# Attention and MLP steps of a chained kernel in a 3 to 2 pattern across block seams, with z of the next batch split two blocks ahead

## The chip, the cores and the metric

One core of one Trainium2 chip runs the whole program. The metric is the device time of one execution in microseconds (us). The engines are PE (TensorE matmuls; PEld is its weight load), DVE (VectorE), ACT (ScalarE), POOL (GpSimd) and SP (SyncE, which issues most DMAs here).

## The reference

Three layers are chained. Everything is float32.

```python
# attention: u, v (8, 3072, 256), z (8, 3072, 64)
attn = np.maximum(z @ z.T / S, 0.0) ** 2
x = u * (attn @ v)                       # then flattened to (24576, 256)
# MLP: w_in (256, 2048), w_out (2048, 256)
h = x @ w_in
x = (h * sigmoid(h)) @ w_out
# routed MLP: 8 experts, w1 (256, 1024), w2 (1024, 256); each row goes to the expert with the largest logit
e = argmax(x @ w_gate); p = softmax(x @ w_gate)[e]
out = p * sigmoid(x @ w_output_gate)[e] * (relu(x @ w1[e]) @ w2[e])
```

## The kernel before

Float32 products are made of three matmuls on split operands: hi is a rounded copy of a tile, lo is what is left, and hi x hi, hi x lo and lo x hi are added up in PSUM. So nearly every tile costs a copy (hi, on ACT mostly) and a subtraction (lo, on DVE).

The 24576 rows are 48 blocks of 512 (TQ). Block n is block q = n % 6 of batch b = n // 6. An **attention block** has 24 steps, one per 128 keys (KT = 24); an **MLP block** has 16 steps, one per 128 hidden columns (NF1 = 16). Step i is an `Item` with a front, which makes hi and lo of its tile, and a back, which multiplies them into an accumulator. The loop at the end of `moe_chain` emits front(i), the lo of step i - 1, and back(i - 3) (LOOK = 3), so PE's order in the program is: front of a step, back of the step three earlier.

A **direct** attention step has two front matmuls (L264, L265), relu (L267), square (L269) and a copy to hi (L271 on ACT or L273 on DVE), lo (L242), and six back matmuls (L289 to L291). The scores are symmetric, so from block 3 on a block q with q > 0 need not compute the tiles against earlier blocks of its batch: such a **mirrored** step loads the stored tile `sym` with four DMAs (L216), transposes it in 32 x 32 blocks on DVE (L223), copies hi (L259) and subtracts lo (L242); it has no front matmul. A direct step whose tile will be needed later stores it to `sym` (L230). An MLP step has six front matmuls (L323), sigmoid (L325, ACT), product (L327, DVE), hi (L330), lo (L332) and twelve back matmuls of 256 columns (L357 to L359).

After the last back of an attention block, `finish` (L302, two instructions) multiplies the accumulator by u into x, and `split_x` makes xh and xl of it (L195, L197). The MLP block n needs both, and the attention block n + 1 needs nothing of them.

The order of steps is written out by hand in the list `order`. From block 3 on it is: seven attention steps of block n (PRE), then sixteen times one MLP step of block n - 1 and one attention step of block n, then the last attention step. So at each seam of two blocks eight attention steps follow each other.

Beside the steps there are tasks: each has a step by which it is due, a step from which it may run, and a cost; `run_tasks` emits a task when it is due, or earlier when the steps' budgets leave credit. Tasks split z and v of a batch (`prep`: hl, hh and ll, vh and vl), transpose mirrored tiles, decode the MLP weights during blocks 0 to 2, and route the rows of a finished MLP block: 32 dot products of 256 columns (L367, each with a read of the accumulator), a selection (L399 to L414), a rank (L425 to L430) and four scatters. Loads for `prep` and for mirrored tiles go through four buffers `raw`, in the order in which the tasks are due, and SP issues all of them.

```python
prep(max(att_step(n, j * NS) - (0 if n else 2), rel), rel, load_zz(b, j), f_hl(j))
prep(att_step(n, 0), att_step(n - 1, KT // 2) if n else 0, load_zz(b, q), f_hh((b, q)))
```

After block 47 come 61 tiles of the routed MLP (L637, L656 and the back matmuls again), which the change leaves as they are but for buffers.

Of the kernel before, what the change touches and what calls it, by code (L numbers as in the profile page):

```python
# [29 lines left out]
PRE = 7  # L30

# [10 lines left out]
def moe_chain(tc, zT, uT, vp, win, wout, w12, wgT, wogT, out):  # L42
# [20 lines left out]
    assert NBLK > 3 and KT >= PRE + NF1 and KT > 2 * PRE and NF1 >= 16 and NA <= P and NB <= P and N // P <= 256  # L63
# [3 lines left out]
    with ExitStack() as ctx:  # L67
# [37 lines left out]
        ident = cp.tile([P, P], F32, name="ident")  # L105
        make_identity(nc, ident)
# [77 lines left out]

        def split_x(b, q, last=False):
            x = xs[(b, q)]
            if last:
                r = mk(cp, [P, NS, RW], F32, "rec", 2).rearrange("p s c -> p (s c)").bitcast(F32R)
                h = [r[:, c * TQ:(c + 1) * TQ] for c in range(ND)]
                l = [mk(cp, [P, TQ], F32R, "x", 2) for c in range(ND)]  # L190
            else:
                h, l = ([t[:, c, :] for c in range(ND)] for t in [mk(cp, [P, ND, TQ], F32R, g, 1) for g in ("xh", "xl")])
# [27 lines left out]
        def flip(b, q, k):  # L220
            def f(t):
                a = flipped[b, q, k] = mk(cp, [P, TQ], F32, "t1", 3)
                nc.vector.transpose(a, t)  # L223
            return f
# [7 lines left out]
        def att_items(b, q, hold):  # L232
# [4 lines left out]
            def front(i):  # L237
# [39 lines left out]
            def back(i):  # L277
                k = ks[i]

                def f():  # L280
# [708 lines left out]
```

## Time and profile before

| what | us |
|---|---|
| median of 3 runs | 5383.55 (5381.29 to 5387.24) |
| the profiled execution's own time | 5386.84 |
| its span, first to last instruction | 5385.1 |
| busy: PE, PEld | 5237.8 (97%), 4536.8 (84%) |
| busy: DVE, ACT, POOL | 3830.7 (71%), 3233.8 (60%), 483.3 (9%) |
| granted TensorE clock, mean | 0.995 |

The span is the time from the first to the last instruction of the profiled execution. A busy time is the sum of the stretches in which at least one instruction of that engine ran. Matmuls overlap, so that PE's busy time is no measure of how densely they stand; the start times in the timeline are. "L290 [1.22 <-DVE lo L242]" behind a row means that the engine was idle for 1.22 us before that instruction, and that the last thing that it waited for was DVE's instruction of line 242.

### The profile page before, as it was taken

What the parts mean: (1) busy time and instruction counts of PE and PEld (TensorE: products, weight loads), DVE (VectorE), ACT (ScalarE), POOL (GpSimd) and SP (SyncE); (2) the same over time, 40 slices, a digit from 0 to 9 for tenths busy, and PEclk for the clock granted to TensorE, in tenths of its full rate; (3) what the DMA queues carried; (4) which work ended last, traced back from release to release, by engine and by line L of the source; (5) the groups of instructions that cost most, each with busy time, mean ns of one, the idle gap of its engine ahead of it and who ended that gap; (6) DMA issues with size and microseconds to landing.
All of it is one profiled execution on the core that took longest, in us unless ns stands there. A gap on an engine that the chain in (4) does not pass through costs nothing.

```text
span 5385.1 us, 88728 instructions
## 1 busy us (share of the span) xinstructions
PE 5237.8 (97%) x30026; PEld 4536.8 (84%) x30026; DVE 3830.7 (71%) x9655; ACT 3233.8 (60%) x5776; POOL 483.3 (9%) x503
## 2 busy tenths in 40 slices
PE   7999999999999999999999999999999999999999
PEld 5888888888878887888888888888888899999998
DVE  8777757776776667676767676677667886666687
ACT  6655665566556655656565556556665555555576
POOL 3100000000000000000000000000000022111111
PEclk9999999999999999999999999999999999999999
DMA  4143323433342334233423342334324456565564
GB/s 149 56 88 77 102 79 81 89 94 83 78 96 82 83 72 106 77 82 71 105 82 77 77 106 85 69 78 109 83 71 76 136 175 202 176 181 176 168 228 160
DMA packets 1335279, 574.38 MB, mean 107 GB/s; under 512 B 1173405, under 2 KB 1206814, under 8 KB 1319072
## 3 DMA queue, kind: packets, MB, share of 16 engines
q1 hardware_dynamic: 1316000, 516.72, 37.7%
q0 software_dynamic: 18816, 51.93, 2.6%
q8 instruction: 237, 3.88, 0.3%
q14 instruction: 226, 1.85, 0.1%
HBM read 391.32 MB, written 178.14 MB: 106 GB/s over the span
## 4 chain that ended last, share of the span: by engine, by line
PE 80%; DVE 9%; ACT 5%; DMA 3%; issue 2%; SPq 0%; DVEq 0%; ACTq 0%; POOL 0%; POOLq 0%
PE ps L323 17%; PE ps L656 10%; PE acc L357 10%; PE acc L359 10%; PE acc L358 10%; PE acc L290 7%; PE acc L291 6%; PE acc L289 6%; DVE lo L242 2%; PE ps L265 2%; PE ps L264 2%; ACT t L269 2%; DVE junk L367 1%; DVE t L223 1%; ACT t L267 1%
## 5 line engine op out<-in xcount | busy, mean ns | idle before, releaser
L327 DVE TENSOR_TENSOR t<-ps,t 128x512 f32<-128x512 f32 x768 | 531.0, 691 | 791.3 <-ACT t L325 756.3
L358 PE MATMUL acc<-woutl,hi 128*128 128x256 f32 x3600 | 1004.8, 279 | 0.0
L290 PE MATMUL acc<-lo,vh 128*128 128x512 f32 x2304 | 922.5, 400 | 82.8 <-DVE lo L242 82.6
L242 DVE TENSOR_TENSOR lo<-t,hi 128x512 fp32r<-128x512 f32 x1152 | 796.8, 693 | 249.9 <-ACT hi L271 249.9
L291 PE MATMUL acc<-hi,vl 128*128 128x512 f32 x2304 | 909.9, 395 | 0.0
L289 PE MATMUL acc<-hi,vh 128*128 128x512 f32 x2304 | 906.4, 393 | 0.0
L330 ACT ACTIVATE hi<-t 128x512 fp32r<-128x512 f32 x768 | 486.0, 633 | 661.8 <-DVE t L327 647.4
L359 PE MATMUL acc<-wouth,lo 128*128 128x256 f32 x3072 | 860.3, 280 | 12.2 <-DVE lo L332 12.1
L357 PE MATMUL acc<-wouth,hi 128*128 128x256 f32 x3072 | 860.1, 280 | 0.0
L325 ACT ACTIVATE t<-ps 128x512 f32<-128x512 f32 x768 | 456.7, 595 | 452.3 <-PE ps L323 450.1
L358 PEld LDWEIGHTS acc<-woutl,hi 128*128 128x128 f32 x3600 | 681.1, 189 | 38.2
L290 PEld LDWEIGHTS acc<-lo,vh 128*128 128x128 f32 x2304 | 435.6, 189 | 234.3 <-DVE lo L242 140.2
L357 PEld LDWEIGHTS acc<-wouth,hi 128*128 128x128 f32 x3072 | 579.6, 189 | 32.6
L359 PEld LDWEIGHTS acc<-wouth,lo 128*128 128x128 f32 x3072 | 583.1, 190 | 16.7 <-DVE lo L332 16.7
L323 PE MATMUL ps<-xl,winh 128*128 128x512 f32 x1504 | 596.3, 396 | 0.2
L323 PE MATMUL ps<-xh,winh 128*128 128x512 f32 x1504 | 592.0, 394 | 0.0
L323 PE MATMUL ps<-xh,winl 128*128 128x512 f32 x1504 | 590.7, 393 | 0.0
L367 DVE CUSTOM_DVE_ANT_0 junk<-rec,wg 128x256 f32<-128x256 f32 x1536 | 570.3, 419 | 0.0
L259 ACT ACTIVATE hi<-t 128x512 fp32r<-128x512 f32 x468 | 296.1, 633 | 427.0 <-DVE t L223 333.3
L433 POOL DMA_INDIRECT scr<-rec,si x192 | 200.8, 1046 | 3850.3 <-DVE si L430 1167.1
L332 DVE TENSOR_TENSOR lo<-t,hi 128x512 fp32r<-128x512 f32 x768 | 518.9, 676 | 24.5
L289 PEld LDWEIGHTS acc<-hi,vh 128*128 128x128 f32 x2304 | 435.8, 189 | 98.0
(444 smaller groups left out, 9770.5 us busy)
## 6 DMA issues: line engine op xcount, KB each, us to landing
raw<-in_w_dram SPq DMA_DIRECT2D x122, 1024.0 KB
sym<-t SPq DMA_DIRECT2D x468, 256.0 KB
raw<-sym SPq DMA_DIRECT2D x1872, 64.0 KB
raw<-in_zT_dram SPq DMA_DIRECT2D x192, 128.0 KB
raw<-in_vp_dram SPq DMA_DIRECT2D x96, 256.0 KB
u<-in_uT_dram SPq DMA_DIRECT2D x96, 256.0 KB
xg<-scr SPq DMA_DIRECT2D x39, 544.0 KB
x<-scr SPq DMA_DIRECT2D x304, 64.0 KB
```

Source lines behind the costliest of these rows:

```text
L242: nc.vector.tensor_tensor(out=lo, in0=a, in1=r32(hi), op=ALU.subtract)
L289: nc.tensor.matmul(acc[:, c, :], h, hi, start=i == 0, stop=False)
L290: nc.tensor.matmul(acc[:, c, :], h, lo, start=False, stop=False)
L291: nc.tensor.matmul(acc[:, c, :], l, hi, start=False, stop=i == KT - 1)
L323: nc.tensor.matmul(ps, win_at(w, c, f_), x[c], start=c == 0 and i == 0, stop=c == ND - 1 and i == 2)
L327: nc.vector.tensor_tensor(out=g, in0=ps, in1=sg, op=ALU.mult)
L332: return lambda: nc.vector.tensor_tensor(out=lo, in0=g, in1=r32(hi), op=ALU.subtract)
L357: nc.tensor.matmul(y[:, s, :], a, wh, start=first and s % per_bank == 0, stop=False, skip_group_check=True)
L358: nc.tensor.matmul(y[:, s, :], a, wl, start=False, stop=False, skip_group_check=True)
L359: nc.tensor.matmul(y[:, s, :], l, wh, start=False, stop=last, skip_group_check=True)
L367: nc.vector.tensor_tensor_reduce(out=j, in0=a, in1=w, scale=1.0, scalar=0.0, op0=ALU.mult, op1=ALU.add, accum_out=res)
L656: nc.tensor.matmul(ps[:, 0:T], w[:, o:o + P], y[c][:, 0:T], start=c == 0 and j == 0, stop=c == ND - 1 and j == 2)
```

## The change

The order from block 3 on is cut into eighths: three attention steps of block n, then two MLP steps, all through, also across the seams. The MLP of block n - 1 starts with the third eighth of block n and ends in the second eighth of block n + 1. So two x are held: even blocks split into xh and xl, odd ones into xo and x. In block 2 the MLP steps of block 1 are mixed 1 to 1. The last two eighths of block 47 have no MLP steps among them.

u is loaded into the tile xf ten steps before the block's end, and finish works in place. relu and square work in place in t1 (four buffers instead of three), t0 is left to sigmoid with one buffer. Of q = 0, a third of the copies to hi is made on DVE instead of half. hl of the next batch is due in blocks n - 2 (four of six), n - 1 and n; hh five steps before the block's first step; v one step earlier than before. The fill for padding is made in xl during block 0 and kept in DRAM (blank), and the identity for the routed MLP's transposes is made when its pool opens.

```diff
-                        later(2, 1.2, finish, 0)
-                        if hold != "held":
-                            later(3, 1.2, lambda: split_x(b, q, hold == "last"), 0)
+                        later(1, 1.2, finish, 0)
+                        later(3, 1.2, lambda: split_x(b, q, hold == "last"), 0)
...
-                h, l = ([t[:, c, :] for c in range(ND)] for t in [mk(cp, [P, ND, TQ], F32R, g, 1) for g in ("xh", "xl")])
+                odd = (b * NQ + q) % 2
+                h, l = ([t[:, c, :] for c in range(ND)] for t in
+                        [mk(ap_ if g == "xo" else cp, [P, ND, TQ], F32R, g, 1) for g in (("xo", "x") if odd else ("xh", "xl"))])
...
-                    r = mk(cp, [P, TQ], F32, "t0", 2)
-                    nc.scalar.activation(r, ps, AF.Relu)
-                    a = mk(cp, [P, TQ], F32, "t1", 3)
-                    nc.scalar.activation(a, r, AF.Square)
-                    if (early and q and k % 2) or (not early and (q or k % 2)):
+                    a = mk(cp, [P, TQ], F32, "t1", 4)
+                    nc.scalar.activation(a, ps, AF.Relu)
+                    nc.scalar.activation(a, a, AF.Square)
+                    if (early and q and k % 2) or (not early and (q or k % 3)):
...
-                    if i == LOOK + 1:
-                        st["u"] = []
-                        for c in range(ND):
-                            ut = mk(ap_, [P, TQ], F32, "u", 2)
-                            nc.sync.dma_start(out=ut, in_=uT[b, q, :, c, :])
-                            st["u"].append(ut)
+                    if i == KT - UAT:
+                        load_u(b, q)
...
             def finish():
-                x = xs[(b, q)] = []
-                for c in range(ND):
-                    x.append(mk(ap_, [P, TQ], F32, "raw", DEPTH) if hold == "last" else mk(cp, [P, TQ], F32, "x", 2))
-                    nc.vector.scalar_tensor_tensor(out=x[c], in0=st["acc"][:, c, :], scalar=AS, in1=st["u"][c], op0=ALU.mult, op1=ALU.mult)
+                for c, x in enumerate(xs[(b, q)]):
+                    nc.vector.scalar_tensor_tensor(out=x, in0=st["acc"][:, c, :], scalar=AS, in1=x, op0=ALU.mult, op1=ALU.mult)
...
-                    sg = mk(cp, [P, TQ], F32, "t0", 2)
+                    sg = mk(cp, [P, TQ], F32, "t0", 1)
...
+        def make_blank():
+            w = TB // P
+            t = r32(mk(cp, [P, ND, TQ], F32R, "xl", 1)).rearrange("p c t -> p (c t)")[:, 0:w * RW].rearrange("p (s c) -> p s c", c=RW)
+            nc.gpsimd.memset(t, 0.0)
+            nc.gpsimd.memset(t[:, :, D + E:D + E + 1], 1.0e6)
+            for dst in (blank, scr[E * CAP:E * CAP + TB, :]):
+                nc.sync.dma_start(out=dst.rearrange("(p s) c -> p s c", p=P), in_=t)
...
+        GA, GM = KT // 8, NF1 // 8
+        owed = []
         for n in range(3, NBLK):
-            order += [("a", n, 0, PRE)]
-            end = NF1 - (PRE if n == NBLK - 1 else 0)
-            for k in range(end):
-                order += [("m", n - 1, k, k + 1), ("a", n, PRE + k, PRE + k + 1)]
-            order += [("a", n, PRE + end, KT), ("m", n - 1, end, NF1)]
-        order += [("m", NBLK - 1, 0, NF1)]
+            for g in range(8):
+                if n > 3 or g >= 2:
+                    j = (g - 2) % 8 * GM
+                    owed.append(("m", n - 1 if g >= 2 else n - 2, j, j + GM))
+                if n < NBLK - 1 or g < 6:
+                    order += owed
+                    owed = []
+                order += [("a", n, g * GA, (g + 1) * GA)]
+        order += owed + [("m", NBLK - 2, 6 * GM, NF1), ("m", NBLK - 1, 0, NF1)]
...
-                    rel = last_use(n - 1, range(j * NS, (j + 1) * NS)) + 1 if n else 0
-                    prep(max(att_step(n, j * NS) - (0 if n else 2), rel), rel, load_zz(b, j), f_hl(j))
-            prep(att_step(n, 0), att_step(n - 1, KT // 2) if n else 0, load_zz(b, q), f_hh((b, q)))
+                    if n:
+                        due = att_step(n - 2, KT // 2 + 2 * j) if j < NQ - 2 else att_step(n - 1, KT // 2) if j < NQ - 1 else att_step(n, KT // 2)
+                        rel = max(last_use(n - t, range(j * NS, (j + 1) * NS)) for t in range(1, NQ + 1)) + 1
+                    else:
+                        due, rel = max(att_step(n, j * NS) - 2, 0), 0
+                    prep(due, rel, load_zz(b, j), f_hl(j))
+            prep(att_step(n, 0) - (5 if n else 0), att_step(n - 1, KT // 2) if n else 0, load_zz(b, q), f_hh((b, q)))
```

How the instructions move shows at three places.

**DVE at the seam of blocks 16 and 17**, before. L223 transposes a mirrored tile, L242 makes lo of an attention step, L302 is finish, L367 a dot product with its read, L197 makes xl:

```order
L223 STREAM_TRANSPOSE t_3866_15760<-raw_15169 128x512
L302 SCALAR_TENSOR_TENSOR x_15767<-acc_14763,u_14790 128x512
L302 SCALAR_TENSOR_TENSOR x_15769<-acc_14763,u_14792 128x512
L242 TENSOR_TENSOR lo_15733<-t_3859_15739,hi_15732 128x512
L367 ISA junk_15786,L_15751<-rec_15691,wg 128x256
L367 ISA L_15751 128x1
L367 ISA junk_15788,L_15751<-rec_15691,wg 128x256
L367 ISA L_15751 128x1
L223 STREAM_TRANSPOSE t_3876_15790<-raw_15217 128x512
L197 TENSOR_TENSOR xl_15798<-x_15767,xh_15797 128x512
L197 TENSOR_TENSOR xl_15798<-x_15769,xh_15797 128x512
L242 TENSOR_TENSOR lo_15776<-t_3866_15760,hi_15775 128x512
```

and in the changed kernel, where the lines are L303 (finish), L251 and L333 (lo of an attention and of an MLP step), L206 (xl), L328 (the MLP's product), and L426 to L431 are the rank of the rows of an earlier block:

```order
L333 TENSOR_TENSOR lo_16262<-t_3757_16259,hi_16261 128x512
L303 SCALAR_TENSOR_TENSOR xf_15823<-acc_15395,xf_15823 128x512 x2
L251 TENSOR_TENSOR lo_16272<-t_3763_16276,hi_16271 128x512
L426 TENSOR_TENSOR t_16314<-ps_16311,ecap 128x32
L427 TENSOR_TENSOR t_16314<-t_16314,oh_16220 128x32
L429 TENSOR_REDUCE sf_16317<-t_16314 128x4
L431 CAST si_16319<-sf_16317 128x4
L251 TENSOR_TENSOR lo_16290<-t_3767_16294,hi_16289 128x512
L206 TENSOR_TENSOR xl_16356<-xf_15823,xh_16355 128x512 x2
L328 TENSOR_TENSOR t_3780_16370<-ps_16361,t_3779_16368 128x512
L251 TENSOR_TENSOR lo_16334<-t_3775_16338,hi_16333 128x512
L328 TENSOR_TENSOR t_3786_16392<-ps_16383,t_3785_16390 128x512
```

Finish and xl stood among mirrored steps, two of their transposes and dot products; now they stand among direct steps and MLP products.

**DVE in a mirrored group of the changed kernel**, further on in block 17 (names as above, L232 is the transpose):

```order
L328 TENSOR_TENSOR t_3804_16479<-ps_16470,t_3803_16477 128x512
L251 TENSOR_TENSOR lo_16451<-t_3797_16443,hi_16450 128x512
L328 TENSOR_TENSOR t_3809_16500<-ps_16491,t_3808_16498 128x512
L333 TENSOR_TENSOR lo_16482<-t_3804_16479,hi_16481 128x512
L232 STREAM_TRANSPOSE t_3812_16512<-raw_16034 128x512
L333 TENSOR_TENSOR lo_16503<-t_3809_16500,hi_16502 128x512
L232 STREAM_TRANSPOSE t_3816_16529<-raw_16059 128x512
L251 TENSOR_TENSOR lo_16520<-t_3812_16512,hi_16519 128x512
```

Before, one product, one lo, one transpose and one lo followed each other in turn; now the second product stands ahead of the first MLP lo (L333).

**ACT at the seam of batches 2 and 3**, before. L168 and L174 make hl and hh of z, L95 vh of v, L259 hi of a mirrored step, L267 and L269 are relu and square of the new batch's first step:

```order
L330 ACTIVATE hi_17553<-t_4297_17551 128x512
L259 ACTIVATE hi_17568<-t_4300_17563 128x512
L259 ACTIVATE hi_17588<-t_4304_17584 128x512
L168 ACTIVATE hl_107<-raw_17482 128x512
L95 ACTIVATE vh_113<-raw_17524 128x512
L174 ACTIVATE hh_17607<-raw_17565 128x512
L267 ACTIVATE t_4316_17618<-ps_17615 128x512
L269 ACTIVATE t_4317_17620<-t_4316_17618 128x512
L95 ACTIVATE vh_114<-raw_17586 128x512
```

and in the changed kernel, with L173 (hh), L264 (hi, mirrored), L326 and L331 (sigmoid and hi of the MLP), L96 (vh), L272 and L273 (relu and square):

```order
L264 ACTIVATE hi_17039<-t_3938_17032 128x512
L173 ACTIVATE hh_17055<-raw_16919 128x512
L326 ACTIVATE t_3948_17072<-ps_17065 128x512
L331 ACTIVATE hi_17076<-t_3949_17074 128x512
L326 ACTIVATE t_3953_17093<-ps_17086 128x512
L331 ACTIVATE hi_17097<-t_3954_17095 128x512
L264 ACTIVATE hi_17111<-t_3957_17107 128x512
L264 ACTIVATE hi_17125<-t_3961_17121 128x512
L264 ACTIVATE hi_17153<-t_3969_17149 128x512
L96 ACTIVATE vh_108<-raw_17059 128x512
L326 ACTIVATE t_3975_17179<-ps_17172 128x512
L331 ACTIVATE hi_17183<-t_3976_17181 128x512
```

hl is gone from the seam. hh was the instruction just ahead of the first relu (L267); now twelve others stand between it and the first relu (L272), which follows the last row shown by two.

## Rows read from the trace of the kernel before

**Rows 1.** The page, part 1: busy time, share, instructions.

```profile
PE 5237.8 (97%) x30026; PEld 4536.8 (84%) x30026; DVE 3830.7 (71%) x9655; ACT 3233.8 (60%) x5776; POOL 483.3 (9%) x503
```

**Rows 2.** Windows, blocks 3 to 47: stretch, length, busy by engine, clock, DMA share, GB/s.

```profile
275.50:4200.00 3924.50, 3825.26 (x20679) 3251.33 (x20678) 2746.24 (x7000) 2368.74 (x3996) 193.71 (x225) 1.00 0.36 85
```

**Rows 3.** Chain of waits (start, length, what), then PE's timeline, in undisturbed stretches.

```profile
1342.65 1.39 PE ps L323 x6
1344.04 0.23 PE acc L289
...
1345.42 0.12 PE acc L357
...
1346.83 1.39 PE ps L323 x6
...
1697.99 1.37 PE ps L323 x6
...
1702.57 1.37 PE ps L323 x6
...
1588.29 0.39 PE L264 MATMUL ps<-hh,hl 128*128 128x512 f32 x1
...
1590.14 0.39 PE L264 MATMUL ps<-hh,hl 128*128 128x512 f32 x1
```

**Rows 4.** PE's timeline at the seam of blocks 14 and 15.

```profile
1330.48 0.39 PE L289 MATMUL acc<-hi,vh 128*128 128x512 f32 x1
1332.09 0.50 PE L290 MATMUL acc<-lo,vh 128*128 128x512 f32 x1 [1.22 <-DVE lo L242]
...
1336.45 0.40 PE L289 MATMUL acc<-hi,vh 128*128 128x512 f32 x1
1337.07 0.50 PE L290 MATMUL acc<-lo,vh 128*128 128x512 f32 x1 [0.22 <-DVE lo L242]
```

**Rows 5.** PE's timeline at the starts of batches 2 and 3.

```profile
1048.52 0.49 PE L264 MATMUL ps<-hh,hl 128*128 128x512 f32 x1 [2.41 <-DVE vl L93]
...
1571.69 0.39 PE L291 MATMUL acc<-hi,vl 128*128 128x512 f32 x1
1575.05 0.80 PE L264 MATMUL ps<-hh,hl 128*128 128x512 f32 x1 [2.98 <-ACT hh L174]
...
1576.37 0.41 PE L357 MATMUL acc<-wouth,hi 128*128 128x256 f32 x1
```

**Rows 6.** Chain of waits at the seam of blocks 14 and 15.

```profile
1330.27 1.17 DVE x L302 x2
...
1332.38 0.34 DVE junk L367
...
1333.35 1.18 DVE xl L197 x2
```

**Rows 7.** Timelines of PE and DVE behind the front of an MLP step.

```profile
1563.56 0.39 PE L289 MATMUL acc<-hi,vh 128*128 128x512 f32 x1
...
1564.44 0.69 DVE L327 TENSOR_TENSOR t<-ps,t 128x512 f32<-128x512 f32 x1 [1.70 <-ACT t L325]
1565.05 0.68 DVE L242 TENSOR_TENSOR lo<-t,hi 128x512 fp32r<-128x512 f32 x1
1565.65 0.70 DVE L223 STREAM_TRANSPOSE t<-raw 128x512 f32<-128x512 f32 x1
1566.28 0.65 DVE L332 TENSOR_TENSOR lo<-t,hi 128x512 fp32r<-128x512 f32 x1
```

**Rows 8.** Groups of ACT: line, count, busy us, mean ns, idle before and its end.

```profile
L269 ACT ACTIVATE t<-t 128x512 f32<-128x512 f32 x684 | 432.7, 633 | 44.8 <-DMA sym<-t 13.9 <-DVE lo L332 5.8 <-ACT t L267 2.3
L267 ACT ACTIVATE t<-ps 128x512 f32<-128x512 f32 x684 | 400.4, 585 | 38.1 <-PE ps L265 37.3
L271 ACT ACTIVATE hi<-t 128x512 fp32r<-128x512 f32 x564 | 356.9, 633 | 18.0
```

**Rows 9.** SP's timeline with a backlog of loads.

```profile
1333.78 11.04 SPq L216 DMA_DIRECT2D raw<-sym  x16
```

More of the change, by code (lines that the diff above doesn't have):

```diff
@@ L183, in moe_chain, with load_u @@
         xs = {}
+        def load_u(b, q):
+            t = mk(cp, [P, ND, TQ], F32, "xf", 1)
+            x = xs[(b, q)] = [t[:, c, :] for c in range(ND)]
+            for c in range(ND):
+                nc.sync.dma_start(out=x[c], in_=uT[b, q, :, c, :])
         def split_x(b, q, last=False):
@@ L344, in f @@
                         later(1, 0, copy(rec, 0), 0)
-                        later(2, 0, copy(rec, 2), 0)
+                        later(1, 0, copy(rec, 2), 0)
                 return f
@@ L498, in f @@
                 r = nc.sync.value_load(fr[0:1, e:e + 1], min_val=0, max_val=E * CAP - TB)
-                nc.sync.dma_start(out=scr[ds(r, TB), :].rearrange("(p s) c -> p s c", p=P), in_=fill)
+                nc.sync.dma_start(out=scr[ds(r, TB), :].rearrange("(p s) c -> p s c", p=P), in_=blank.rearrange("(p s) c -> p s c", p=P))
                 padded.append(e)
@@ L524, in final_tables @@
                 later(4 + NF2 * e, 0.0, pad(fr, e))
-        fill = cp.tile([P, TB // P, RW], F32, name="fill")
-        def make_fill():
-            nc.gpsimd.memset(fill, 0.0)
-            nc.gpsimd.memset(fill[:, :, D + E:D + E + 1], 1.0e6)
-            nc.sync.dma_start(out=scr[E * CAP:E * CAP + TB, :].rearrange("(p s) c -> p s c", p=P), in_=fill)
+        blank = dram.tile([TB, RW], F32, name="blank")
+        def make_blank():
[5 more added lines that the diff above has]
+                nc.sync.dma_start(out=dst.rearrange("(p s) c -> p s c", p=P), in_=t)
         bstack = ExitStack()
@@ L574, in f @@
                 r = nc.sync.value_load(tabs[kind][t:t + 1, 0:1], min_val=0, max_val=E * CAP + TB - T)
-                st["xb"] = [mk(cp, [P, TQ], F32, "x", 2) for _ in range(ND)]
+                t_ = r32(mk(cp, [P, ND, TQ], F32R, "x", 1))
+                st["xb"] = [t_[:, c, :] for c in range(ND)]
                 for c in range(ND):
@@ L636, in f @@
                     for s in range(T // P):
-                        nc.tensor.transpose(ps[:, s * P:(s + 1) * P], st["xg"][:, s, c * P:(c + 1) * P], ident)
+                        nc.tensor.transpose(ps[:, s * P:(s + 1) * P], st["xg"][:, s, c * P:(c + 1) * P], bp["i"])
                 split(ps[:, 0:T], st["yh"][c][:, 0:T], st["yl"][c][:, 0:T], m2_at[i])
@@ L694, in moe_chain @@
         blocks = [(b, q) for b in range(B) for q in range(NQ)]
-        order = [("a", 0, 0, KT), ("a", 1, 0, KT), ("a", 2, 0, PRE), ("m", 0, 0, NF1), ("a", 2, PRE, 2 * PRE), ("m", 1, 0, NF1), ("a", 2, 2 * PRE, KT)]
-        for n in range(3, NBLK):
-            order += [("a", n, 0, PRE)]
-            end = NF1 - (PRE if n == NBLK - 1 else 0)
-            for k in range(end):
-                order += [("m", n - 1, k, k + 1), ("a", n, PRE + k, PRE + k + 1)]
-            order += [("a", n, PRE + end, KT), ("m", n - 1, end, NF1)]
-        order += [("m", NBLK - 1, 0, NF1)]
+        order = [("a", 0, 0, KT), ("a", 1, 0, KT), ("a", 2, 0, PRE), ("m", 0, 0, NF1)]
+        for k in range(NF1):
+            order += [("a", 2, PRE + k, PRE + k + 1), ("m", 1, k, k + 1)]
+        order += [("a", 2, PRE + NF1, KT)]
+        GA, GM = KT // 8, NF1 // 8
+        owed = []
+        for n in range(3, NBLK):
+            for g in range(8):
[7 more added lines that the diff above has]
+        order += owed + [("m", NBLK - 2, 6 * GM, NF1), ("m", NBLK - 1, 0, NF1)]
         steps = {}
         for n, bq in enumerate(blocks):
-            steps["a", n] = att_items(*bq, {1: "held", NBLK - 1: "last"}.get(n))
+            steps["a", n] = att_items(*bq, "last" if n == NBLK - 1 else None)
             steps["m", n] = moe_items(*bq)
@@ L728, in prep, with used, last_use @@
             stream.append((due, rel, len(stream), load, use, since))
-        def last_use(n, keys):
+        def used(n, keys):
             o = key_order(*blocks[n])
             return max(att_step(n, o.index(k)) for k in keys)
+        def last_use(n, keys):
+            direct = [k for k in keys if not mirrored(*blocks[n], k)]
+            return used(n, direct) if direct else 0
         def f_hl(j):
@@ L795, in moe_chain @@
         tmp = wgt
-        t_val = tmp[:, 2 * TQ:3 * TQ], fill.rearrange("p s c -> p (s c)")[:, 0:TQ]
+        t_val = tmp[:, 2 * TQ:3 * TQ], mk(cp, [P, TQ], F32, "junk", 1)
         t_rem = tmp[:, 3 * TQ:4 * TQ]
```

27 lines of the change are left out of this document (14 added, 13 removed).

## The prediction

> **What bounds the kernel now.** I read the engines' busy times first, then the windows, then the timeline of PE and, where PE paused, that of DVE. PE is busy 97% of the span [rows 1]; the blocks in which attention and MLP steps run together take 3924.5 us of it and keep PE busy 3825.3 us at a granted clock of 1.00 [rows 2]. So PE is the bound, and what can be won is its pauses. A busy share hides part of them, because matmuls overlap (0.39 us long, 0.23 us apart); I count from start to start.
>
> The undisturbed pace: six MLP front matmuls, one mirrored attention step and the twelve MLP back matmuls repeat every 4.18 us (1342.65 to 1346.83), the mirrored step being 1.38 us of it (1344.04 to 1345.42) [rows 3]. With a direct step instead, the pair takes 4.58 us, and a direct step alone 1.85 us (1588.29 to 1590.14) [rows 3]. So an MLP step is 2.80 or 2.73 us of PE.
>
> The pauses stand in one place, the seam of two blocks, where eight attention steps follow each other without an MLP step. In the rows of one seam PE starts a matmul of L290 1.61 us after the one before it, and later another 0.62 us after, where 0.23 us is due; both wait for DVE's lo of L242 [rows 4]. That is 1.8 us, and about 2 with the slower matmuls behind each pause. At the seam of two batches it is worse: PE waits 3.36 us for hh, whose z was loaded too late, and the next two matmuls take 1.32 us instead of 0.46 [rows 5]: 4.0 us for that alone.
>
> One batch, from its first L264 to that of the next, is 1048.52 to 1575.05, 526.5 us [rows 5]. Its work is 96 MLP steps, 60 mirrored and 84 direct ones: 60 x 1.38 + 84 x 1.85 = 238.2, and 96 x 2.73 to 2.80 = 262.1 to 268.8 us. So PE loses 19.5 to 26.2 us per batch; weighted by partners it would be 23, and I take 22, as the pauses that I can point at are five of 2 and one of 4 or more. Seven whole batches (blocks 6 to 47) and the three seams of blocks 3 to 5 make 7 x 22 + 7 = **161 us**, in the range 143 to 190. The other pauses lie in blocks 0 and 1 and at the ends, where the order stays.
>
> **The change, part by part.**
>
> *Even mixing.* It removes no matmul. In the lead of a block DVE had, in the twelve rows shown of before, a transpose 0.63, finish 1.17, xl 1.18, a second transpose, two lo of 0.60 and two dot products of 0.34 [rows 6, 7]: 5.5 us, against two or three mirrored steps of 1.38 us, at most 4.1 us of PE. This is the 1.8 us pause. In the new order finish and xl stand in a stretch of three direct and two MLP steps, 3 x 1.85 + 2 x 2.73 = 11.0 us of PE. The twelve rows there cost DVE 1.17 + 1.18 + two products of 0.61 + four lo of 0.60 + four small ones, at most a dot product each: 7.3 us. Cover is left over, so the regular pause goes. What if the cover is gone? Then DVE is late by the difference and PE pauses for it, as before.
>
> *A mirrored group* (two MLP, three mirrored steps) is 2 x 2.80 + 3 x 1.38 = 9.74 us of PE. DVE has three transposes 0.63, three lo 0.60, two products 0.61, two MLP lo of 0.65 [rows 7] and four to six dot products: 6.2 + 2.1 = 8.3 us. It fits, with 1.4 us to spare. A direct group: ACT has 3 x (0.585 + 0.633 + 0.633) [rows 8] and four MLP instructions of the same lengths, 5.6 + 2.5 = 8.1 of 11.0 us.
>
> *z of the next batch.* hh is made five steps before its use, four of the six hl two blocks earlier, so the 4.0 us of the batch seam should go as well. What is paid: hl costs DVE 0.6 us each, and two can fall in one mirrored group: 8.3 + 1.2 = 9.5 of 9.74 us. It fits barely.
>
> *What I book as remaining.* Nothing in the trace shows the new groups, so I bound it: 0 us (all fits, by the sums above) to half of 161 us (if bursts inside a group cost what seams cost). I take 0.25 us for each of 45 seams, 1.2 us per batch for hl, 0.7 us per batch seam: **24 us**, near the lower end, because the nearest rows, the 1:1 mix of mirrored steps, ran at exactly 4.18 us a pair with DVE almost as full.
>
> *Buffers.* relu and square now work in one of four buffers t1, instead of t0 and the last of three t1. ACT's squares waited 13.9 us in all for the store of sym, most of it in blocks 0 and 1 [rows 8]. The store now has four steps less one relu, instead of three. Bounds: 0 to 13.9 us saved; I take **3**, since DVE decodes weights there and is late anyway. sigmoid's single t0 is free once the product (0.61 us) is done, and the next sigmoid comes 2.7 us later: nothing.
>
> *u into xf, in place:* loaded 13 steps before finish; the same two transfers: nothing. *blank:* two transfers on SP that wait for one POOL memset, with only stores queued behind: nothing, at most 2 us. *ident later, one junk buffer, dots on the same engine:* nothing. *A third instead of half of the casts of q = 0 on DVE:* 28 of them move to ACT, which has 2.9 us spare per direct group: nothing. *The end:* a47 ends with six mirrored steps in a row (DVE 1.23 of 1.38 us each) and 24 MLP steps alone instead of 23: nothing, at most 2 us.
>
> *SP.* Each mirrored step needs four loads of 64 KB, and three steps now come in a burst. Sixteen loads, that is four steps, were issued in 11.04 us where SP had a backlog [rows 9]: 2.76 us a step, while a mirrored group gives 9.74 / 3 = 3.25 us. Four raw buffers carry the burst. I book nothing. The Trainium skill (Perfetto Trace Analysis, section What "DMA-bound" means) says that a kernel can be bound by the issuing engine's sequencer, and that its track is then solid with DMA slices. In these rows the track is solid for that stretch, so the trace agrees that SP can be full, though not that it holds PE up. If the rule held here, the sum would lose what the second rival below loses.
>
> **Sum.** The profiled execution took 5386.84 us: 5386.8 - 161 + 24 - 3 = 5246.8. It stood 3.3 us above the median of the runs, 5383.55, so I forecast **5244 us** for a median. A measurement can tell about 0.2% (10.8 us) from no change.
>
> **Rivals.**
> 1. *Half the pauses stay.* DVE's bursts only move: three transposes and three lo in a row, then pick and dot products before the next product. For it: DVE is 8.3 of 9.74 us full, and 9.5 where hl falls. Against it: the sums above. 80 us stay: 5386.8 - 81 - 3 - 3.3 = 5300 us.
> 2. *SP's issue sets the pace of mirrored groups.* With the stores of sym and u between the loads, a step could need 3.3 us or more instead of 2.76. At 3.31 us each of 468 mirrored steps loses 0.06: 28 us, 5272 us. The gain is gone only at 3.25 + 140/468 = 3.55 us.
> 3. *Two MLP steps in a row starve PE* (slower). On DVE the second product stands before the first lo, and it waits for a sigmoid after the second front. From the next matmul behind a front (1563.56) to the place where such a lo would end (1565.05 + 0.68) are 2.17 us [rows 7]; PE gives two attention backs and two hi matmuls, 2 x 1.38 + 0.23 = 2.99 us. So 0.82 us is spare. If the three ACT instructions of a direct step (1.85 us [rows 8]) stand ahead of the sigmoid, the pair pauses 1.03 us. Some 210 of 360 pairs follow direct steps: 216 us, 5460 us. It decides from 140/210 = 0.67 us a pair, that is 1.49 us in front of the sigmoid. Against it: 2.7 us of other matmuls run ahead of each front, in which ACT empties.
> 4. *It does nothing:* the seams' work is as late as before at another place; about 5384 us.
>
> **Chances.** Forecast 0.66, first rival 0.14, second 0.10, third 0.06, fourth 0.04. Faster is the sum of the first three, 0.90; same 0.04; slower 0.06. Low end: no remainder and all waits for stores gone, 5386.8 - 161 - 13.9 - 3.3 = 5209. High end: the first rival with its rounding, 5303; this leaves out the last two rivals and part of the first.
>
> **What would show it.** PE at the seams: L290 starts 0.23 us after L289, no wait for lo of L242 above 1 us outside blocks 0 and 1, no wait for hh above 1 us. A batch takes about 507 us instead of 526.5. Mirrored groups at 9.7 us, direct at 11.0. Wrong if PE pauses repeat inside groups: waiting for L333's lo (third rival), for a transpose whose raw came late (second), or for L251's lo (first).

## The result, and the profile after

The changed kernel took 5293.82 us (median of 4 runs, 5291.53 to 5296.77) against 5385.4 us for the kernel before on the same chip (4 runs): ratio 0.983, 95% interval 0.9813 to 0.9847, a gain of 91.6 us. The forecast was 5244 us, a gain of 140. The time lies in the range (5209 to 5303), near its high end, and the sign is right; a third of the gain didn't come.

The page of the changed kernel, part 1, answers to [rows 1]:

```profile
PE 5189.7 (98%) x30026; PEld 4529.6 (86%) x30026; DVE 3897.6 (74%) x9627; ACT 3234.9 (61%) x5804; POOL 491.2 (9%) x503
```

The same matmuls ran. DVE's busy time rose by 67 us, although the change adds hardly any work there; the dot products explain that below.

One batch, as a window over the changed kernel from the first L293 of block 12 to that of block 18 (columns as in [rows 2]):

```profile
1031.10:1540.70 509.60, 505.84 (x2773) 434.54 (x2772) 374.24 (x934) 319.77 (x546) 26.24 (x30) 1.00 0.36 88
```

Between the same matmuls it took 526.2 us before (526.5 from first front to first front [rows 5]); 507 were forecast. PE's waits, first the four largest before, then all after (in total, times, longest, us):

```profile
PE acc L290 <- DVE lo L242: 82.6, 103, 3.1
PE ps L264 <- ACT hh L174: 19.6, 6, 6.1
PE ps L264 <- DVE hl L169: 13.1, 7, 1.9
PE acc L359 <- DVE lo L332: 12.1, 20, 1.5
```

```profile
PE acc L360 <- DVE lo L333: 42.4, 35, 23.8
PE acc L294 <- DVE lo L251: 37.5, 34, 2.5
PE ps L269 <- ACT hh L173: 6.8, 1, 6.8
PE ps L324 <- DVE xl L206: 1.9, 1, 1.9
```

The attention lo's waits more than halved. hh is waited for once, at the start of the program. What is new is the first row: 23.8 us in one piece.

The waits alone hide that matmuls behind a pause are slow, so I counted PE's lost time as in the prediction, from start to start: for every PE instruction the distance to the next start, less the median distance behind its line, distances within 8 ns of the median left out. For each profiled execution, in us (per block: mean over 7 batches, blocks 6 to 47). The last column is the median of all runs; the profiled execution lies within 4 us of it, but for the row "order and z put back", where it is the fastest of 11 (5374.89):

| kernel | q = 0 | q = 1, 2, 3 each | q = 4 | q = 5 | blocks 6 to 47 | blocks 0 to 2 | after block 47 | median of runs |
|---|---|---|---|---|---|---|---|---|
| before | 5.42 | 2.33 | 2.33 | 6.57 | 149 | 45.3 | 4.0 | 5385.4 |
| changed | 3.50 | 0.10 | 1.93 | 0.28 | 42 | 46.0 | 32.1 | 5293.8 |
| order and z put back | 3.98 | 1.74 | 1.73 | 6.66 | 123 | 46.2 | 4.8 | 5383.6 |
| the same, junk in halves | 4.00 | 1.13 | 1.13 | 6.19 | 103 | 47.1 | 3.9 | 5353.0 |
| order put back | 3.08 | 1.74 | 1.76 | 1.95 | 84 | 46.9 | 4.8 | 5335.8 |
| z put back | 4.13 | 0.08 | 0.09 | 4.31 | 61 | 46.6 | 33.4 | 5318.6 |
| casts moved | 4.58 | 0.10 | 1.88 | 0.27 | 49 | 45.4 | 32.0 | 5299.9 |
| casts behind the lo | 2.07 | 0.08 | 1.84 | 0.30 | 31 | 46.9 | 33.3 | 5283.8 |
| hl spread | 3.43 | 0.08 | 0.92 | 0.27 | 34 | 46.6 | 31.7 | 5285.5 |
| junk in halves | 2.76 | 0.09 | 0.83 | 0.10 | 28 | 47.4 | 29.2 | 5275.0 |
| routing earlier | 3.39 | 0.09 | 1.91 | 1.52 | 50 | 47.1 | 5.0 | 5275.2 |
| four edits | 1.75 | 0.09 | 0.09 | 0.90 | 21 | 45.9 | 4.0 | 5239.5 |
| four edits, v later | 1.29 | 0.09 | 0.09 | 0.90 | 18 | 47.0 | 4.0 | 5236.6 |

**The regular seam** is as forecast. The first backs of block 15 of the changed kernel stand 0.23 us apart; before, 1.61 us lay between two of its early backs [rows 4]. PE's timeline, then DVE's at the start of that block (start, length, instruction, its idle time before and the releaser):

```profile
1295.42 0.40 PE L293 MATMUL acc<-hi,vh 128*128 128x512 f32 x1
1295.65 0.40 PE L294 MATMUL acc<-lo,vh 128*128 128x512 f32 x1
```


```profile
1290.56 1.29 DVE L303 SCALAR_TENSOR_TENSOR xf<-acc,xf 128x512 f32<-128x512 f32 x2 [0.45 <-PE acc L295]
1291.76 0.68 DVE L251 TENSOR_TENSOR lo<-t,hi 128x512 fp32r<-128x512 f32 x1
1293.04 0.69 DVE L251 TENSOR_TENSOR lo<-t,hi 128x512 fp32r<-128x512 f32 x1 [0.60 <-ACT hi L275]
1295.38 1.29 DVE L206 TENSOR_TENSOR xl<-xf,xh 128x512 fp32r<-128x512 f32 x2 [1.65 <-ACT xh L204]
```

Between finish and xl DVE now waits for others, 0.60 and 1.65 us, where before the chain of waits ran on DVE from finish to xl [rows 6]. The groups run at the forecast pace: from the first front of a pair to the first front of the next, the median is 9.61 us for 100 mirrored groups (9.74 expected) and 11.07 for 174 direct ones (11.0).

**Three places lose time.** First, the start of q = 0. PE, DVE and ACT of the changed kernel, block 18, three timelines:

```profile
1549.29 0.28 PE L359 MATMUL acc<-woutl,hi 128*128 128x256 f32 x1
1550.46 0.39 PE L360 MATMUL acc<-wouth,lo 128*128 128x256 f32 x1 [0.90 <-DVE lo L333]
```

```profile
1549.38 0.43 DVE L277 CAST hi<-t 128x512 fp32r<-128x512 f32 x1 [1.69 <-ACT t L273]
1549.72 0.69 DVE L333 TENSOR_TENSOR lo<-t,hi 128x512 fp32r<-128x512 f32 x1
```

```profile
1547.06 1.14 ACT L96 ACTIVATE vh<-raw 128x512 fp32r<-128x512 f32 x2
1548.10 0.58 ACT L272 ACTIVATE t<-ps 128x512 f32<-128x512 f32 x1
1548.71 0.63 ACT L273 ACTIVATE t<-t 128x512 f32<-128x512 f32 x1
```

DVE's lo of the MLP is ready to run, but a copy to hi of the next attention step stands ahead of it and waits 1.69 us for ACT's square, which waits for two vh. This pause isn't new. In the kernel before, block 18 has the same; there the copy waits 1.31 us, until ACT's square (1604.62 to 1605.25) is done (PE, then DVE):

```profile
1606.37 0.39 PE L359 MATMUL acc<-wouth,lo 128*128 128x256 f32 x1 [0.88 <-DVE lo L332]
```

```profile
1605.29 0.43 DVE L273 CAST hi<-t 128x512 fp32r<-128x512 f32 x1 [1.31 <-PE ps L265]
1605.63 0.68 DVE L332 TENSOR_TENSOR lo<-t,hi 128x512 fp32r<-128x512 f32 x1
```

Of the 5.42 us that q = 0 lost before, 2.4 us come with a wait for hl near its start, and about 3 us are pauses inside the block, such as this one. The change left these standing.

Second, q = 4, block 16 (PE, then DVE):

```profile
1431.59 0.40 PE L293 MATMUL acc<-hi,vh 128*128 128x512 f32 x1
1433.07 0.50 PE L294 MATMUL acc<-lo,vh 128*128 128x512 f32 x1 [1.08 <-DVE lo L251]
```

```profile
1425.14 0.69 DVE L168 TENSOR_TENSOR hl<-raw,hl 64x512 fp32r<-64x512 f32 x1 [0.71 <-ACT hl L167]
...
1427.07 0.41 DVE L368 CUSTOM_DVE_ANT_0 junk<-rec,wg 128x256 f32<-128x256 f32 x1
...
1427.52 0.42 DVE L368 CUSTOM_DVE_ANT_0 junk<-rec,wg 128x256 f32<-128x256 f32 x1
...
1431.00 0.69 DVE L168 TENSOR_TENSOR hl<-raw,hl 64x512 fp32r<-64x512 f32 x1 [0.73 <-ACT hl L167]
...
1432.33 0.68 DVE L251 TENSOR_TENSOR lo<-t,hi 128x512 fp32r<-128x512 f32 x1
```

Each of the two hl makes DVE wait 0.7 us for ACT's half of it, beside its own 0.6, and four dot products stand between them, 0.46 us from start to start, where one took 0.34 before [rows 6].

Third, once, the end. PE, then the chain of waits of the changed kernel (start, length, what):

```profile
4098.56 0.28 PE L359 MATMUL acc<-woutl,hi 128*128 128x256 f32 x1
4122.62 0.58 PE L360 MATMUL acc<-wouth,lo 128*128 128x256 f32 x1 [23.78 <-DVE lo L333]
```

```profile
4096.53 11.12 DMA xg<-scr
...
4108.45 0.99 POOL scr L434
...
4111.17 2.44 DMA scr<-rec,si
...
4117.09 2.47 DMA scr<-rec,si
...
4120.16 0.59 ACT rec L350
...
4121.28 0.70 DVE t L328
```

The loads of routed rows (xg) of tiles 0 and 1 stand ahead of block 45's four scatters (L434) and read the tensor that these write. The scatters wait for them, and go out one after another. The copy of block 46's rows (L350) needs one of two rec buffers: the other holds x of block 47. A sigmoid stands behind the copy on ACT, then product, lo and PE wait.

### The profile page after: what moved, and what is told of

The parts are those of the page before. It is cut to its first block, busy times and chain, and to the rows that moved or that the text cites. A ratio compares the mean times of both kernels' runs of the same rounds, so it can differ in the third digit from the quotient of the medians.

```text
span 5292.0 us, 88328 instructions
## 1 busy us (share of the span) xinstructions
PE 5189.7 (98%) x30026; PEld 4529.6 (86%) x30026; DVE 3897.6 (74%) x9627; ACT 3234.9 (61%) x5804; POOL 491.2 (9%) x503
## 4 chain that ended last, share of the span: by engine, by line
PE 84%; DVE 8%; ACT 3%; issue 2%; DMA 2%; SPq 0%; POOL 0%; DVEq 0%; ACTq 0%; POOLq 0%
PE ps L324 17%; PE ps L663 10%; PE acc L360 9%; PE acc L358 9%; PE acc L359 9%; PE acc L295 8%; PE acc L294 8%; PE acc L293 8%; PE ps L269 3%; PE ps L270 3%; DVE lo L251 1%; DMA raw<-sym 1%; DVE lo L333 1%; DVE junk L368 1%; DVE t L328 1%
## 5 line engine op out<-in xcount | busy, mean ns | idle before, releaser
L328 DVE TENSOR_TENSOR t<-ps,t 128x512 f32<-128x512 f32 x768 | 529.4, 689 | 655.5 <-ACT t L326 649.8
L331 ACT ACTIVATE hi<-t 128x512 fp32r<-128x512 f32 x768 | 486.0, 633 | 764.1 <-DVE t L328 764.1
L294 PE MATMUL acc<-lo,vh 128*128 128x512 f32 x2304 | 911.1, 395 | 37.7 <-DVE lo L251 37.5
L295 PE MATMUL acc<-hi,vl 128*128 128x512 f32 x2304 | 910.9, 395 | 0.0
L293 PE MATMUL acc<-hi,vh 128*128 128x512 f32 x2304 | 903.3, 392 | 0.0
L360 PE MATMUL acc<-wouth,lo 128*128 128x256 f32 x3072 | 858.5, 279 | 42.5 <-DVE lo L333 42.4
L251 DVE TENSOR_TENSOR lo<-t,hi 128x512 fp32r<-128x512 f32 x1152 | 791.4, 688 | 130.9 <-ACT hi L275 128.9
L368 DVE CUSTOM_DVE_ANT_0 junk<-rec,wg 128x256 f32<-128x256 f32 x1536 | 648.7, 422 | 35.3
L326 ACT ACTIVATE t<-ps 128x512 f32<-128x512 f32 x768 | 454.6, 592 | 265.5 <-PE ps L324 263.7
L434 POOL DMA_INDIRECT scr<-rec,si x192 | 206.7, 1077 | 3767.2 <-DVE lo L251 1705.9
L264 ACT ACTIVATE hi<-t 128x512 fp32r<-128x512 f32 x468 | 295.8, 632 | 418.7 <-DVE t L232 333.9
L333 DVE TENSOR_TENSOR lo<-t,hi 128x512 fp32r<-128x512 f32 x768 | 523.6, 682 | 13.1 <-issue 0.2
L293 PEld LDWEIGHTS acc<-hi,vh 128*128 128x128 f32 x2304 | 434.2, 188 | 98.8
L295 PEld LDWEIGHTS acc<-hi,vl 128*128 128x128 f32 x2304 | 434.3, 189 | 91.4
L666 ACT ACTIVATE hi<-ps 128x512 fp32r<-128x512 f32 (+1 forms) x488 | 254.7, 522 | 396.9 <-PE ps L663 375.3
L668 DVE SCALAR_TENSOR_TENSOR lo<-ps,hi 128x512 fp32r<-128x512 f32 (+1 forms) x488 | 288.2, 591 | 245.8 <-ACT hi L666 244.0
```

Source lines behind the costliest of these rows:

```text
L251: nc.vector.tensor_tensor(out=lo, in0=a, in1=r32(hi), op=ALU.subtract)
L293: nc.tensor.matmul(acc[:, c, :], h, hi, start=i == 0, stop=False)
L294: nc.tensor.matmul(acc[:, c, :], h, lo, start=False, stop=False)
L295: nc.tensor.matmul(acc[:, c, :], l, hi, start=False, stop=i == KT - 1)
L328: nc.vector.tensor_tensor(out=g, in0=ps, in1=sg, op=ALU.mult)
L333: return lambda: nc.vector.tensor_tensor(out=lo, in0=g, in1=r32(hi), op=ALU.subtract)
```

## The experiments

Nearly all are single edits of the changed kernel, 4 to 11 runs each (5 mostly) beside the kernel before.

**1. The end: loads of rows later.**

```diff
-            task(lo_, lo_, 0, m2_load(i))
+            if i < 2:
+                task(lo_, lo_, 0, m2_load(i, (0,)))
+                task(b_open + 6, b_open + 6, 0, m2_load(i, (1,)))
+            else:
+                task(lo_, lo_, 0, m2_load(i))
```

> The changed kernel, with the loads of the gathered rows (xg) of routed tiles 0 and 1 issued six steps later, behind the four scatters of block 45; their weights are loaded where they were. Theory: the pause of 24 us at 4098.56 comes from these loads, which stand ahead of block 45's scatters and read the tensor that the scatters write; scatter, copy to rec, product, lo, PE wait for one another in a chain. Then the pause falls below 2 us, and the time by 22 to 28 us, to 5266 to 5272. Rival A: rec with its two buffers is the cause in itself, since the memset of rec and block 46's dot products stand so late that the next copy must wait whatever the scatter does: the pause shrinks by less than half, 5282 to 5294. Rival B: the rows are then late for tile 0 and PE pauses there as long: 5290 to 5296.

5285.66 us (5285.15 to 5287.64), ratio 0.9815 (0.9802 to 0.9829): 8.2 us less, within rival A. PE and POOL:

```profile
4114.08 0.58 PE L360 MATMUL acc<-wouth,lo 128*128 128x256 f32 x1 [15.15 <-DVE lo L333]
```

```profile
4092.91 1.28 POOL L434 DMA_INDIRECT scr<-rec,si  x1 [81.05 <-DVE t L328]
4101.35 0.98 POOL L434 DMA_INDIRECT scr<-rec,si  x1 [7.16 <-DMA scr<-rec,si]
```

The scatters no longer wait for loads, but they start only at 4092.9: block 45's rank is late by itself. My reading named one link of the chain, worth a third of the pause.

**2. The end: routing of block 45 earlier.**

```diff
+            if n == NBLK - 3:
+                due -= 12
             route_tasks(n, due, rel)
```

> The changed kernel, with the routing of block 45 due twelve steps earlier, so that its dot products, selection and rank are through by the end of attention block 47; nothing else moves but what stands behind it. Moving the row loads took 8.1 us off the time and left a pause of 15 us at the same place. Theory: what is left is the routing of block 45 itself, whose rank comes 80 us after the copy of its rows where 62 to 70 us were usual, with MLP block 46 ending after 85 us instead of 87 to 93 and the other buffer of rec held by x of block 47. With the routing ahead, scatters land before block 46's copy, and also stand ahead of the row loads: the whole pause goes, 22 to 28 us, 5266 to 5272. Rival: the four scatters one after another (3 to 4 us each) and the dot products pressed into the end of block 47 stop PE there for as long: 5278 to 5294.

5275.24 us (5273.83 to 5277.19), ratio 0.9792 (0.9779 to 0.9806): 18.6 us less. The 24 us pause is gone (5.0 us lost after block 47), and the scatters stand ahead of the loads. Between theory and rival lies one new pause, for a count of rows that I had left due with the selection:

```profile
4054.17 0.40 PE L295 MATMUL acc<-hi,vl 128*128 128x512 f32 x1
4061.81 0.17 PE L375 MATMUL ps<-ohc,ones 128*128 128x8 bf16 x1 [7.24 <-DVE ohc L414]
```

**3 and 4. z and order, each put back.** For z the lines that begin with - in the change, for the order likewise.

> The changed kernel with the due times of hl and hh of before (hl in the batch's own blocks, hh at the block's first step). Theory: the early split removed the wait for hh at the batch seams, 4.0 us, and with it the slow matmuls behind; hl goes back into groups that have cover. Seven batch seams: 28 us back, less some 10 us of the pauses in blocks q = 4, where hl now falls with dot products: 5305 to 5325, with a wait for hh above 2 us at 7 seams. Rival: the even mixing alone covers hh, and the early hl only costs: 5280 to 5292.

5318.59 us (5314.07 to 5319.8), ratio 0.9873 (0.9858 to 0.9888): 24.8 us more. The seven batch seams are back at 3.15 us from L295 to L269, waiting for hl (19.2 us in 7 waits), not for hh as I expected, and q = 4 loses 0.09 instead of 1.93 us: what the early hl costs there is seen, and what it wins is more.

> The changed kernel with the hand-written order of before from block 3 on (seven attention steps, then one to one, the last attention step), everything else as changed (u into xf, four buffers for relu and square, one for sigmoid, early z). Theory: the mixing removed the pauses of about 2 us at 38 seams inside batches, 76 to 90 us, and brought the 24 us pause at the end, which goes again: 5293.8 + 76 to 90 - 24 - up to 10 (pauses of q = 0 and q = 4 in the new groups) = 5335 to 5360, with pauses for lo of L251 of 1.2 to 1.6 us at the seams and no wait above 3 us after 4000 us. Rival: the seams were freed by finish working in place on xf and by the splits being asked for later, not by the mixing: 5262 to 5295.

5335.81 us (5333.39 to 5338.41), ratio 0.9908 (0.9893 to 0.9923): 42 us more, and no pause at the end. Without the 27 us of the end the order is worth 69, a little below the 76 expected, but not all of that is pauses. The regular seam came back at 1.74 instead of 2.33 us, and the count finds only some 43 us of pauses more. The other 26 us lie between the pauses: with the counted pauses taken off, blocks 3 to 47 take 3743 us in the changed kernel, 3769 to 3771 in the three runs with the old order, and 3758 in the kernel before. Matmuls stand a little further apart there; the median behind L293, the first back, is 0.231 instead of 0.226 us from block 3 on. The order makes this difference; by what, no run shows.

**5. Both put back.** Of the change, the buffers, the casts, v, the earlier finish and splits, and the mixing in block 2 stay.

> The changed kernel with both the hand-written order and the due times of hl and hh of before; what stays of the change is the buffers (u into xf, t1 and t0, one junk buffer), the casts of q = 0, v one step earlier, blank and ident. With the order alone put back it was 5335.8, with the due times alone 5318.6, with neither 5293.8. Theory: the two parts are worth their sum, 42 + 25 = 67 us, and the rest of the change some 20 to 25 us by itself (finish in place and without a task's delay: regular seams 1.75 instead of 2.33 us): 5355 to 5366. Rival: order and z cover one another's waits, so that the last one taken away costs more than alone, and the rest is worth nothing: 5375 to 5392.

5383.56 us (5374.89 to 5387.71, 11 runs), ratio 0.9994 (0.9985 to 1.0003): the rival's range. Its first half is seen: late z costs 47.8 us in the old order (5335.8 to 5383.6) and 24.8 in the new one, so order and z cover one another's waits. Its second half, that the rest is worth nothing, is not so plain: the regular seams lose 0.6 us less each, yet the time is that of before. Part of it is the wider distance between the pauses, 3770 against 3758 us, and another small part may cost as much as these seams win. The next run looks for that part.

**6. Both put back, dot products on two halves of one tile.**

```diff
-            j = mk(cp, [P, TQ], F32, "junk", 1)[:, 0:D]
+            halves[0] ^= 1
+            j = junkt[:, halves[0] * D:halves[0] * D + D]
```

> The changed kernel with the order and the due times of hl and hh of before, and the dot products on two halves of one tile: one edit against the run that put both back (5383.6, the same as before). Theory: there the one junk buffer takes back what the other small parts win (regular seams 1.73 instead of 2.33 us); without it 8 to 20 us less, 5363 to 5376. Rival: in the old order DVE has room between dot products, the buffer costs nothing there, and its 19 us in the changed kernel come from the new order alone: 5379 to 5388.

5353.01 us (5349.42 to 5355.03) where before took 5379.81, ratio 0.995 (0.9936 to 0.9963). Against the ratio of run 5 that is 0.0044, or 24 us: more than expected. The one junk buffer had eaten most of what the other small parts win. Between the profiled executions of this run and of before, some 47 us of pauses are gone and 34 us of time; the wider distances between the pauses take the rest back.

**7. The same edit on the changed kernel.**

> The changed kernel with the dot products writing the two halves of one junk tile in turn instead of the same half each time. Theory: with one buffer each dot waits for the one before it (0.46 us from start to start instead of 0.345), 8 pairs and more a block that cost DVE 0.12 us each; spacing goes back to 0.34 to 0.36 us, DVE busy falls by 50 to 90 us, and PE gains only where DVE is late, in q = 4 and at the end: 0 to 8 us less, 5286 to 5294. Rival: the wait is between a dot and its read of the accumulator, so nothing changes: spacing 0.46, 5291 to 5296.

5275.0 us (5273.66 to 5275.99), ratio 0.9792 (0.9779 to 0.9806): 18.8 us less, more than twice the theory's most. The groups of dot products (count, busy us, mean ns) before, changed, and with halves:

```profile
L367 DVE CUSTOM_DVE_ANT_0 junk<-rec,wg 128x256 f32<-128x256 f32 x1536 | 570.3, 419 | 0.0
```

```profile
L368 DVE CUSTOM_DVE_ANT_0 junk<-rec,wg 128x256 f32<-128x256 f32 x1536 | 648.7, 422 | 35.3
```

```profile
L372 DVE CUSTOM_DVE_ANT_0 junkt<-rec,wg 128x256 f32<-128x256 f32 x1536 | 569.4, 420 | 0.4
```

An instruction takes the same 420 ns; with one buffer each waits for the one before it instead of overlapping its end. A block q = 4 now loses 0.83 us (1.93 in the changed kernel), a block q = 0 2.76 (3.50), and the end 3 us less.

**8 and 9. Copies of q = 0.** First the second of three steps copied on DVE (k % 3 == 1), then the copy emitted with the lo of its step:

```diff
                 def low(a, hi, lo, cast=False):
                     def f():
+                        if cast:
+                            nc.vector.tensor_copy(hi, a)
                         nc.vector.tensor_tensor(out=lo, in0=a, in1=r32(hi), op=ALU.subtract)
```

> The changed kernel where DVE makes the copy to hi of the second of every three steps of q = 0 instead of the first. Theory: in the blocks q = 0 the copy of the first step stands ahead of the MLP's lo on DVE and waits for ACT's square, which stands behind two vh; PE pauses 0.6 to 1.2 us three times a block for that lo, 3.3 us in each of 7 blocks. With the second step's copy on DVE the first step's hi comes from ACT and the MLP's lo goes ahead: 8 to 18 us less, 5276 to 5286. Rival: ACT is what is late there (vh, relu, square), so PE pauses as long, now for hi or lo of the attention step: 5290 to 5297.

5299.88 us (5298.74 to 5301.47), ratio 0.9841 (0.9828 to 0.9855): slower by 6 us, the rival's side and past it. PE waits there now for the attention step's own lo:

```profile
PE acc L294 <- DVE lo L251: 45.5, 53, 2.4
PE acc L360 <- DVE lo L333: 35.6, 26, 23.8
```

> The changed kernel, where DVE's copies to hi in the blocks q = 0 are emitted together with the lo of the same step, one step later, so that they stand behind the MLP's lo instead of ahead of it; as many on DVE as before. Theory: the pauses of q = 0 (3.5 us in each of 7 blocks) are PE waiting for the MLP's lo, which stands behind a copy that waits for ACT's square. They fall to under 1 us: 15 to 24 us less, 5270 to 5279. Rival: ACT itself is late at the start of q = 0, as the worse time with the second step's copies on DVE suggests (5299.9); then PE waits as long for hi or lo of the attention step: 5288 to 5300.

5283.78 us (5283.09 to 5286.26), ratio 0.9809 (0.9795 to 0.9822): 10 us less, between the two. Of 3.5 us a block 2.07 stay: the MLP's lo is free (31.7 us of waits, of which 23.6 are the end), and a later pause for the attention's lo, with vh ahead of relu and square on ACT, is what is left. Both theories hold a part.

**10. hl three steps apart.** `att_step(n - 2, KT // 2 - 3 + 3 * j)` for `+ 2 * j`.

> The changed kernel with the four early hl due three attention steps apart instead of two, so that no two fall into one mirrored group. Theory: the pause of 1.3 us for lo of L251 and the 0.6 us beside it in each block q = 4 come from two hl subtractions (0.6 us each) with dot products in one group of 9.7 us. Seven blocks times 1 to 1.8 us: 7 to 13 us less, 5281 to 5287. Rival: it is not the two but any one of them with the dots, so the pause stays or splits in two: 5290 to 5297.

5285.5 us (5283.03 to 5288.78), ratio 0.9813 (0.9799 to 0.9826): 8.3 us less, as expected; q = 4 loses 0.92 instead of 1.93 us.

**11 and 12. Together.** Runs 2 (with the count six steps later), 7, 9 and 10; then v due at `att_step(n, 2 * j) + 1` as well.

> The changed kernel with four edits together: the routing of block 45 due twelve steps earlier (with the count of rows for the first table six steps later than that, so that PE doesn't stand 7.6 us for it), the dot products on two halves of one tile, the four early hl three steps apart, and DVE's copies of q = 0 behind the MLP's lo. Theory: the pauses are separate, so the gains add up but for q = 4, where halves and spreading treat the same pause: 18.6 + 7 (the count's pause) + 18.8 + 8.3 - 6 + 10 = 57 us less, 5232 to 5246. Rival: DVE is one queue, and room won at one place is used up at the next, so half is seen: 5255 to 5270.

5239.5 us (5239.26 to 5241.96), ratio 0.9728 (0.9714 to 0.9741): 54.3 us less than the changed kernel, in the theory's range.

> The four edits together, and v of the next batch due two steps later (one step behind the keys that need it instead of one ahead; its backs come three steps behind), so that vh stands behind relu and square at the start of q = 0. Theory: the pause that is left there (1.2 us for lo of L251's kind, with vh ahead of the square on ACT) goes: 7 x 1 to 2 us less than with the four edits alone. Rival: vh and vl are then late for the backs themselves, or fall on the sigmoid: no better, or up to 10 us worse than the four edits.

5236.6 us (5235.8 to 5237.67), ratio 0.9721 (0.9708 to 0.9735): 2.9 us less again, below the 7 expected. This version beats both kernels, 150 us below before. Its page, part 1, and the main waits that are left:

```profile
PE 5173.9 (99%) x30026; PEld 4523.6 (86%) x30026; DVE 3814.1 (73%) x9627; ACT 3248.6 (62%) x5804; POOL 492.9 (9%) x503
```

```profile
PE acc L297 <- DVE lo L253: 34.9, 35, 3.7
PE ps L271 <- ACT hh L173: 6.1, 1, 6.1
```

Most of what is left, 47 us, lies in blocks 0 to 2, where the change mixes anew only the MLP steps of block 1.

## Why the prediction was right in sign and range, and 50 us off

| term of the sum | forecast | in the profiled runs |
|---|---|---|
| pauses of blocks 3 to 47 gone | -161 | -160.9 |
| what remains in them | +24 | +48.0 |
| wait of the squares for sym (pauses of PE in blocks 0 to 2) | -3 | +0.7 |
| the end | nothing, at most 2 | +28.1 |
| not in the sum | | -9.0 |
| together | -140 | -93.1 (5386.84 to 5293.77) |

**The pauses' price was right, as a remainder of span less work.** The same count gives 160.9 us for blocks 3 to 47 of the kernel before, 161 in the forecast. But the pauses that the prediction pointed at, five of 2 and one of 4, make only 14 of its 22 us a batch. The count shows where the rest was: q = 5 and q = 0 lose 12.0 us together, 9.7 beside one regular seam, not 4.0. Beside the wait for hh there are slow matmuls for 3.35 us behind it (last section), the second wait, for hl, and the pauses inside q = 0. That the other pauses came from eight attention steps in a row, and at the batch seam from late z, was right: order and z put back bring most of them back (1.74 of 2.33 us at a regular seam), and with the change q = 1, 2, 3 and 5 lose only 0.10 to 0.28 us. Which of finish, xl and the transposes costs what was not tried one by one; the dot products count, as a seam goes from 1.74 to 1.13 us with halves.

**The remainder was mis-sized, 48 for 24:** 24.5 us in q = 0, 13.5 in q = 4, 4 in the other blocks of the seven batches, 6 in blocks 3 to 5. Two steps failed. The first booked all of the 161 us as gone but for a guessed remainder, although some 3 us of pauses in each block q = 0 were of a kind that the change left standing. "A third instead of half of the casts of q = 0 on DVE: ... nothing" counted ACT's room over a group and not the order on DVE's queue, where a copy stands ahead of a lo: 10 us come back by moving copies behind. What the third instead of half is worth by itself no run shows. The second, "It fits barely" for two hl in one mirrored group left out that DVE waits 0.7 us for ACT's half of each; spreading them gives 8 us.

**"one junk buffer ... nothing" was the worst of the small terms:** 18.8 us here, about 24 in the old order. The prediction priced a dot product at the 0.34 us between two of them before; that distance held because the next one wrote another buffer. This cost overlaps the remainder, as it lengthens the same bursts.

**"The end: ... nothing, at most 2 us" cost 28.1:** 24 us of pause, some 2.7 of slower matmuls behind it (granted clock 0.50 from 4123 to 4127 us), the rest small. I had looked only at PE's and DVE's room in the last steps, and not at who holds rec and at what stands ahead of the scatters on POOL, though moving MLP block 45's end by eight steps moves its routing too. Moving the routing alone removed it; moving the loads alone removed a third.

**The 3 us for the squares' wait** did not show in the time. ACT's wait for the store of sym fell from 13.9 to 2.4 us, but PE's pauses in blocks 0 to 2, where most of that wait was, are as long as before.

**The rivals.** The time is nearest to that of the first (5300), but by another way: in the blocks that it speaks of 48 of 161 us stay, not half. One of its signs is there, though: PE waits 1.0 to 1.1 us for L251's lo in seven of the blocks q = 4. The third, two MLP steps in a row starving PE, exists in small: the waits for the MLP's lo are 42.4 - 23.8 = 18.6 us, not 216, 13.6 of them in q = 0, where the pause shown stands behind a copy, not behind a sigmoid. The second is not seen: mirrored groups run at 9.61 us, under the 9.74 of the sums, and q = 5, which has most of them, loses 0.28 us. By the rule of the Trainium skill (Perfetto Trace Analysis, section What "DMA-bound" means) SP's sequencer could have been the bound; these rows speak against it here. The fourth is out by the interval.

**Luck.** The 9 us that the sum has no term for are slightly shorter distances between matmuls outside the pauses. The run with the old order put back shows that the order makes them; I did not follow by what. Without them the time would have been 5303 us, the very end of the range, so that it lies inside is partly luck.

## What to carry to other kernels

Sums of busy time over a group told rightly which seams would close; what they missed was order within one queue: a short copy that waits for another engine, put ahead of work that is due. When work ends earlier or later in a program, follow its buffers to their last reader, here rows, scatters and the loads of the next phase, before calling the end free. A scratch output that nobody reads still needs two buffers if its writers follow one another.

## What was not expected of the hardware

A pause of PE can cost more than its length. In the version with four edits and v later PE pauses once for 4.13 us (4022.79 to 4026.92), and its matmuls then stand 0.43 us apart instead of 0.23. PE's timeline, then windows over that stretch and the next (the clock is the third figure from the end):

```profile
4028.48 0.63 PE L296 MATMUL acc<-hi,vh 128*128 128x512 f32 x1
4028.90 0.63 PE L297 MATMUL acc<-lo,vh 128*128 128x512 f32 x1
```

```profile
4028.00:4031.00 3.00, 3.00 (x8) 2.32 (x7) 2.45 (x5) 1.49 (x3) 0.00 (x0) 0.50 0.00 0
4031.50:4036.00 4.50, 4.50 (x22) 3.68 (x21) 1.29 (x2) 1.73 (x3) 0.00 (x0) 1.00 0.00 0
```

The granted clock is 0.50, the lower level of 1.2 GHz, for some 3 us, beginning 0.8 us behind the pause: about 1.4 us more. The kernel before had such stretches behind the waits for z: at the start of batch 3, behind the 3.36 us for hh, the granted clock is 0.50 from 1575.05 to 1578.40, and matmuls of 256 columns stand 0.21 us apart instead of 0.11. Ten such stretches lie between 288 and 4101 us before, and none in the changed kernel, so part of what early z wins is clock. The pauses of 1 to 1.5 us inside blocks show no such stretch; there only the first matmul is longer (0.50 against 0.39 us).
